# Sink attention and a feed-forward mixer on one core: zero products leave the plan and fill planned gaps of TensorE, and the whole order is searched anew

## The chip, the core and the metric

The kernel runs on one core of one Trainium2 chip. The metric is the device time of one execution in microseconds (us), as the median of several runs. Engines are called as in the profile: PE is TensorE's matmul stream and PEld its weight loads, DVE is VectorE, ACT ScalarE, POOL GpSimd, SP SyncE (here: the queue from which nearly all DMAs are issued).

## The reference

Four batches of 8 heads, 768 positions and 64 channels go through attention with 4 sink positions and a window of 128, then a low-rank mix over positions and a feed-forward layer of 512 to 2048 to 512, with a residual.

```python
scores = scale * q @ k.T                  # (4, 8, 768, 768)
keep = (pos_k < n_sink) | ((0 <= rel) & (rel < window))
a = softmax(where(keep, scores, -1e9))    # + 1e-9 under the quotient
x = (a @ v)                               # heads side by side: (4, 768, 512)
u = x + (x.T @ U @ V).T                   # U (768, 32), V (32, 768): over positions
out = u + relu(u @ w_ch1) @ w_ch2         # 512 -> 2048 -> 512
```

The weights U, V, w_ch1 and w_ch2 come as 64-bit floats and are narrowed on the chip.

## The kernel before

All of the fast path is recorded first as steps (class Plan): each step has an engine, or several that could run it, a planned duration, the tiles it reads and writes, and a priority. Tiles come from rings of buffers; the eight PSUM banks are such a ring (`self.bank`), and a step that is the first to write a bank "takes" it. `Plan.forward` then plays the steps through a list scheduler: each engine takes, at the time at which it is free, the ready step of the lowest priority number. `Plan.order` plays this some rounds, keeps the priorities of the shortest play, and applies a list of random shakes (SEEDS: a seed and a number of turns each). The steps are issued in the order of their planned starts; on the chip each engine runs its own steps in that order and waits for semaphores, so the plan fixes the order and the chip the times.

The work runs in stages on PE:

- Twelve products of a zero tile with itself (`spin`, L1643) at the start, before the branch.
- Batch 0's attention in plain 32-bit products for pairs of heads: scores (L708), softmax (L762 and L764 on DVE, L769 on ACT), transposes of the probabilities (L825), the triangular selects on POOL (L848, L851), the product with v (L732). Then the mix: transposes back to rows (L989), scaling into `wsum` (L998 on DVE), the product with U (L1000) into a bank whose copy is `t` (L521 on ACT, then the low part by the subtraction L1043 on DVE), and the product of `t` with V (L1067).
- The feed-forward layers of batches 0, 1 and 2 (L1305 to L1307 into `hh`, `hl`, then L1326), with the next batch's attention and mix woven between; batch 0's also narrows the weights, piece by piece: seven steps per piece on DVE and ACT (L115 to L123), then the halves of `w` (L521, L528). The first pieces are needed when the first feed-forward step begins.
- The last batch's feed-forward by a scheme of seven products in place of eight (L1194, L1263), and its outputs (L1282 and DMAs).

In `Fast.run`, 40 further zero products (NIDLE) are planned as ordinary steps of PE: 0.22 us each, each takes a PSUM bank of its own, priority 1e6, so that the scheduler sets one wherever PE has nothing else ready, until the 40 are used up. Each writes 128 by 128 zeros into its bank, and nothing reads them.

Of the kernel before, what the change touches and what calls it, by code (L numbers as in the profile page):

```python
# [10 lines left out]
F32 = mybir.dt.float32  # L11
# [11 lines left out]
P = 128  # L23
# [11 lines left out]
CH = 384  # L35
NCHUNK = S // CH
NBLK = CH // P
# [7 lines left out]
VC = 384  # L45
RAW = 2 * DM + 2
NSPIN = 12
NIDLE = 40
TRI = ()
ROUNDS = 10  # L50
SEEDS = ((300016, 1), (300037, 1), (300043, 1), (300076, 1), (300095, 1), (300109, 1), (300118, 1), (300125, 1), (300139, 1), (300193, 1), (300202, 1), (300209, 1), (300262, 1), (300430, 1), (300467, 1), (300473, 1), (300497, 1), (300521, 1), (300569, 1), (300586, 1), (300667, 1), (300733, 1), (300788, 1), (300838, 1), (300853, 1), (300869, 1), (300955, 1), (301207, 1), (301253, 1), (301256, 1), (301310, 1), (301379, 1), (301439, 1), (301478, 1), (301519, 1), (301685, 1), (301813, 1), (301850, 1), (301985, 1), (302191, 1), (302354, 1), (303016, 1), (303143, 1), (303320, 1), (303350, 1),)
SAME = 0.0842
PRICE = {"DVE": 3.0, "ACT": 1.5, "POOL": 1.5}
NBANK = 8
# [203 lines left out]
class Plan:  # L258
# [13 lines left out]
    def add(self, eng, dur, fn, *args, port=False, **kw):  # L272
        return self.any({eng: (dur, fn, port)}, *args, **kw)
# [102 lines left out]
    def forward(self):  # L376
        avail = dict.fromkeys(self.SYNC, 0.0)
        ready = {e: [] for e in avail}
        port = 0.0
        dma = max((-s.lat - LAND for s in self.steps if s.lat < 0.0), default=0.0)  # L380
        lanes = list(EARLY)

        def release(s):
            for e in s.ways:
                ready[e].append(s)

        def at(s, e):
            t = s.ready[e]
            if e == "SP" and s.lat >= 0.0 and len(lanes) >= NLANE:
                t = max(t, lanes[-NLANE] + 0.03)  # L390
            if s.ways[e][2]:
                t = max(t, port)
            if s.takes:
                n = len(s.takes)
                free = sorted(f[0] for f in s.takes[0].ring.free)
                return max(t, free[n - 1] if len(free) >= n else 1e12)
            return t

        def elsewhere(s, e, end):

            for x, (dur, _, _) in s.ways.items():
                if x != e:
                    t = max(avail[x], at(s, x))
                    queue = sum(o.ways[x][0] for o in ready[x]
                                if (o.prio, o.n) < (s.prio, s.n) and at(o, x) <= t and len(o.ways) == 1)
                    if t + queue + dur * PRICE[x] < end - 1e-9:
                        return True
            return False

        for s in self.steps:  # L410
            s.left, s.ready, s.heirs = len(s.deps) + len(s.after), dict.fromkeys(s.ways, 0.0), []
            for b in s.takes:
                b.ring.free = [(0.0, None, i) for i in range(b.ring.n)]
        for s in self.steps:
            if not s.left:
                release(s)
        done = 0
        while done < len(self.steps):
            turn = sorted((max(avail[e], min(at(s, e) for s in lst)), e) for e, lst in ready.items() if lst)
            turn = [x for x in turn if x[0] < 1e11] or turn  # L420
            pick = None
            for t, e in turn:
                can = sorted((s for s in ready[e] if at(s, e) <= t + 1e-9), key=lambda s: (s.prio, s.n))
# [12 lines left out]
            s.dur, s.fn, lock = s.ways[e]  # L436
            if lock:
                port = t + s.dur
            avail[e] = t + s.dur
            end = t + s.dur + s.lat  # L440
            if e == "SP" and s.lat < 0.0:
                end = -s.lat
            elif e == "SP":
                dma = max(dma, t + s.dur + BEGIN) + s.lat
                end = dma + LAND
                lanes.append(end)
            for b in s.takes:
                slot = min(b.ring.free, key=lambda f: f[0])
                b.ring.free.remove(slot)
                for x in slot[1].steps if slot[1] else ():  # L450
                    x.heirs.append(s)
                b.until, b.open, b.slot = 0.0, len(set(b.steps)), slot[2]
            for b in set(s.gives):
                b.until, b.open = max(b.until, end + 0.25), b.open - 1
                if not b.open:
                    b.ring.free.append((b.until, b, b.slot))
            for u in s.users:
                u.left -= 1
                for x in u.ways:
                    u.ready[x] = max(u.ready[x], end + self.SYNC[e][x])  # L460
                if not u.left:
                    release(u)
            for u in s.followers:
                u.left -= 1
                for x in u.ways:
                    u.ready[x] = max(u.ready[x], t)
                if not u.left:
                    release(u)
            done += 1
        self.span = max(avail.values())  # L470


def mm(n, k=1):
    return k * max(n * 1.085 + 6, 262) / 2400.0
# [18 lines left out]
class Fast:  # L493
# [197 lines left out]
    def attend_pair(self, b, pr, half, t0, qk, v, xT):  # L691
# [41 lines left out]
                        pa()[i * D:(i + 1) * D, c0 * P:(c0 + hi - lo) * P], flat()[:, at:at + D], f32(mv),  # L733
                        start=j == 0, stop=j == len(mms) - 1, skip_group_check=True)
        both = [(xT, (half, 0)), (xT, (half, 1))]
        add("PE", (0.0, 1.25, 1.50)[len(mms) - 2], run, r=ts + [t] + both, w=(pa,), prio=t0)
        self.copy(CH, lambda: xT()[:, half * CH:(half + 1) * CH], lambda: pa()[:, :CH], psum=True, r=(pa,), w=both, prio=t0)

    def scores(self, half, t0, qs, kh, kl, qbase=0, kbase=0):
# [78 lines left out]
    def transposes(self, half, t0, p, whole, own=None, late=True):  # L818
# [4 lines left out]
        def mms():  # L823
            for u in range(NBLK):
                nc.tensor.transpose(tr()[:, u * P:(u + 1) * P], p()[:, u, NS:], self.ident)  # L825
        add("PE", mm(P, NBLK), mms, r=[p] + res, w=(tr,), prio=t0)
        v3 = lambda: tr()[:, :CH].rearrange("p (u j) -> p u j", u=NBLK)
        top = lambda: res[0]()[:, :, 1, :]
        as_ = f32 if whole else lambda ap: ap
# [26 lines left out]
    def values(self, h, half, t0, t, vhl, xT):  # L856
# [4 lines left out]
        for part in range(len(t)):  # L861
            mms = []
            for kb in range(max(half * NBLK - 1, 0), (half + 1) * NBLK):
                lo = 2 * (kb - half * NBLK) + 1
                hi = min(lo + 2, 2 * NBLK)
                lo = max(lo, 0)
                mms.append((kb, lo, hi, max(kb - half * NBLK, 0)))

            def run(part=part, mms=mms):
                for i, (kb, lo, hi, c0) in enumerate(mms):  # L870
                    mv = t[part]().rearrange("p u s j -> p (u s j)")[:, lo * P:hi * P]
                    out = pa()[:, c0 * P:(c0 + hi - lo) * P]
                    st = vhl()[:, kb - kb0].rearrange("p s d -> p (s d)")
                    nc.tensor.matmul(  # L874
                        out, st, mv,
                        start=part == 0 and i == 0, stop=part == len(t) - 1 and i == len(mms) - 1,
                        skip_group_check=True)
            add("PE", (0.0, 0.275, 0.385)[len(mms) - 2], run, r=(t[part], vhl, (xT, (half, hh))), w=(pa,), prio=t0)
        dst = lambda: xT()[hh * D:(hh + 1) * D, half * CH:(half + 1) * CH]
        tb = self.tb()  # L880
        self.copy(CH, tb, lambda: pa()[D:P, :CH], psum=True, r=(pa,), w=(tb,), prio=t0)
# [61 lines left out]
    def mix_half(self, b, half, t0):  # L943
# [25 lines left out]
                pool=False, r=(tr,), w=(pst,), prio=t0)  # L969
        for pr in range(0 if native else NPAIR):  # L970
            ps = self.bank()
            add("PE", mm(CH), lambda ps=ps, pr=pr: nc.tensor.matmul(
                ps()[:, :CH], vs()[:, pr, :], pst()[:, :CH], start=True, stop=True),
                r=(vs, pst), w=(ps,), prio=t0)
            add("DVE", dve(CH), lambda ps=ps, pr=pr, sl=sl: nc.vector.tensor_tensor(
# [410 lines left out]
    def run(self):  # L1386
# [50 lines left out]
        self.bank = Ring(NBANK, lambda i: self.banks[i], free=True)  # L1437

        self.mixers()
        zero = nc.const_aps.tensor(0.0, [P, P], F32)  # L1440
        for _ in range(NIDLE):
            box = self.bank()
            self.plan.add("PE", 0.22, lambda box=box: nc.tensor.matmul(box()[:, :P], zero, zero, start=True, stop=True),  # L1443
                          w=(box,), prio=1e6)
        self.plan.lead = LEAD0
        for half in range(2):
            self.attention_halves(0, half)
# [32 lines left out]
        self.wtiles += [self.pool.tile([P, 4, DM], F32R, name=f"w{i}") for i in range(NRES + NSTREAM)]  # L1480
        for i in range(NP):
            tiles.append(self.pool.tile([P, NBLK, SW + SW], F32, name=f"p{i}"))
        with tc.manual_schedule():
            for s in order:
                s.fn()


# [246 lines left out]
```

## Time and profile before

| | |
|---|---|
| median of 3 runs | 738.07 us (737.06 to 739.82) |
| the profiled execution | 739.45 us, of which 737.7 us span from the first to the last instruction |
| PE busy | 726.3 us, 98% of the span, 4076 matmul records |
| DVE, ACT, POOL busy | 65%, 48%, 26% of the span |
| granted TensorE clock, mean | 0.996 |

The span is read in stages. A plain 32-bit matmul of the program shows as two records in the trace (a zero product too), so 40 zero products are 80 records. Successive matmuls overlap in the records, so the duration of one (399 ns for 512 columns) is longer than the distance to the next; a stretch of the timeline or of the chain of waits gives the distance.

### The profile page before, as it was taken

What the parts mean: (1) busy time and instruction counts of PE and PEld (TensorE: products, weight loads), DVE (VectorE), ACT (ScalarE), POOL (GpSimd) and SP (SyncE); (2) the same over time, 40 slices, a digit from 0 to 9 for tenths busy, and PEclk for the clock granted to TensorE, in tenths of its full rate; (3) what the DMA queues carried; (4) which work ended last, traced back from release to release, by engine and by line L of the source; (5) the groups of instructions that cost most, each with busy time, mean ns of one, the idle gap of its engine ahead of it and who ended that gap; (6) DMA issues with size and microseconds to landing.
All of it is one profiled execution on the core that took longest, in us unless ns stands there. A gap on an engine that the chain in (4) does not pass through costs nothing.

```text
span 737.7 us, 11904 instructions
## 1 busy us (share of the span) xinstructions
PE 726.3 (98%) x4076; PEld 631.4 (86%) x4076; DVE 477.5 (65%) x1343; ACT 352.9 (48%) x1026; POOL 195.3 (26%) x308
## 2 busy tenths in 40 slices
PE   9999999999999999999999999999999999999996
PEld 7678877878787999989899999999988998889895
DVE  7989788898998566578942575655679524122223
ACT  6675375675873455547641265455554222121120
POOL 4340030312431264465330045544424000000000
PEclk9999999999999999999999999999999999999999
DMA  8685767757675377554585898752368945475433
GB/s 300 229 292 203 236 241 265 251 187 265 224 264 197 110 269 255 194 187 155 196 295 176 288 323 273 268 185 80 128 204 278 316 160 200 147 290 191 171 114 119
DMA packets 45958, 160.95 MB, mean 218 GB/s; under 512 B 5056, under 2 KB 11712, under 8 KB 35648
## 3 DMA queue, kind: packets, MB, share of 16 engines
q1 hardware_dynamic: 45600, 159.71, 62.5%
q8 instruction: 34, 0.56, 0.3%
q10 hardware_dynamic: 288, 0.39, 0.2%
q14 instruction: 36, 0.29, 0.1%
HBM read 119.97 MB, written 40.11 MB: 217 GB/s over the span
## 4 chain that ended last, share of the span: by engine, by line
PE 91%; DVE 5%; DMA 2%; ACT 1%; issue 1%; DVEq 0%; ACTq 0%
PE bank L1326 25%; PE bank L1305 9%; PE bank L1306 9%; PE bank L1307 8%; PE bank L1263 8%; PE bank L1194 8%; PE bank L708 4%; PE bank L874 3%; PE bank L732 3%; PE bank L825 3%; PE bank L752 2%; PE bank L753 2%; PE bank L1443 1%; DMA w<-wd 1%; PE bank L989 1%; PE bank L1000 1%
## 5 line engine op out<-in xcount | busy, mean ns | idle before, releaser
L1326 PE MATMUL bank<-w,hh 128*128 128x512 f32 x576 | 183.5, 399 | 0.0
L1305 PE MATMUL bank<-ul,w 128*128 128x384 f32 x384 | 134.3, 350 | 0.7 <-ACT first1k L521 0.7
L1306 PE MATMUL bank<-uh,w 128*128 128x384 f32 x384 | 129.9, 338 | 0.1
L1307 PE MATMUL bank<-uh,w 128*128 128x384 f32 x384 | 129.4, 337 | 0.0
L1326 PE MATMUL bank<-w,hl 128*128 128x512 f32 x288 | 113.6, 395 | 1.0 <-DVE hl L1316 1.0
L1326 PEld LDWEIGHTS bank<-w,hh 128*128 128x128 f32 x576 | 102.9, 188 | 12.7 <-issue 1.4
L769 ACT ACTIVATE p<-p,ms 128x132 f32<-128x132 f32 x192 | 76.3, 399 | 48.9 <-DVE ms L764 48.0
L1316 DVE SCALAR_TENSOR_TENSOR hl<-bank,hh 128x384 fp32r<-128x384 f32 x96 | 53.0, 552 | 63.5 <-ACT hh L1313 63.1
L1313 ACT ACTIVATE hh<-bank 128x384 fp32r<-128x384 f32 x87 | 42.6, 489 | 80.1 <-PE bank L1307 79.3
L1305 PEld LDWEIGHTS bank<-ul,w 128*128 128x128 f32 x384 | 72.2, 188 | 9.6 <-issue 2.7
L1306 PEld LDWEIGHTS bank<-uh,w 128*128 128x128 f32 x384 | 72.3, 188 | 5.5 <-DVE w L528 0.5
L1307 PEld LDWEIGHTS bank<-uh,w 128*128 128x128 f32 x384 | 72.1, 188 | 0.0
L1326 PEld LDWEIGHTS bank<-w,hl 128*128 128x128 f32 x288 | 54.1, 188 | 14.1 <-DVE hl L1316 1.4
L764 DVE CUSTOM_DVE_ANT_0 p<-bank,mask 128x132 f32<-128x132 f32 x192 | 50.9, 289 | 13.9 <-PE bank L753 12.1
L762 DVE COPY_PREDICATED bank<-past,bank 128x128 f32<-128x128 int32 x160 | 41.9, 290 | 4.5 <-PE bank L708 3.7
L792 POOL TENSOR_TENSOR p<-p,r 128x396 f32<-128x396 f32 x16 | 14.0, 874 | 106.9 <-DVE r L780 106.8
L1263 PE MATMUL bank<-w,ul 128*128 128x512 f32 x144 | 38.5, 395 | 0.0
L769 ACT ACTIVATION_READ_ACCUMULATOR p<-p,ms 128x1 f32 x192 | 36.2, 189 | 0.0
L790 ACT ACTIVATE p<-p,r 128x132 f32<-128x132 f32 x96 | 31.4, 394 | 3.6 <-DVE r L780 3.4
L530 POOL TENSOR_TENSOR kl<-qkraw,kh 128x792 fp32r<-128x792 f32 x10 | 21.2, 2118 | 42.4 <-ACT kh L521 19.2
L848 POOL TENSOR_SCALAR_AFFINE_SELECT oph<-oph 128x256 fp32r<-128x256 f32 (+3 forms) x48 | 25.1, 523 | 24.2 <-ACT oph L521 24.1
L1263 PEld LDWEIGHTS bank<-w,ul 128*128 128x128 f32 x144 | 26.9, 188 | 5.1
(242 smaller groups left out, 1433.0 us busy)
## 6 DMA issues: line engine op xcount, KB each, us to landing
w<-wd SPq DMA_DIRECT2D x56, 1024.0 KB, 5.5
big<-in_w_dram SPq DMA_DIRECT2D x32, 512.0 KB, 4.6
wd<-w SPq DMA_DIRECT2D x16, 1024.0 KB, 4.5
big<-xd SPq DMA_DIRECT2D x33, 256.0 KB, 3.5
sd<-wsum SPq DMA_DIRECT2D x16, 512.0 KB, 7.0
w<-sd SPq DMA_DIRECT2D x8, 1024.0 KB, 5.9
qkraw<-in_kk_dram SPq DMA_DIRECT2D x16, 396.0 KB, 5.4
qkraw<-in_qq_dram SPq DMA_DIRECT2D x16, 384.0 KB, 4.4
```

Of the source, the lines that this page charges most:

```text
L762: add("DVE", dve(P), lambda: nc.vector.copy_predicated(st()[:, P + NS:UW], words(self.past), st()[:, 0:P]), w=(st,), prio=t0)
L764: add("DVE", dve(SW), lambda: nc.vector.tensor_tensor_reduce(p()[:, u, :], st()[:, wd - SW:wd], self.mask[:, min(qb, 2), :], -0.125, 3.0e3 ...
L769: add("ACT", act(SW) + 0.22, lambda: nc.scalar.activation(p()[:, u, :], p()[:, u, :], AF.Exp, bias=sm()[:, j:j + 1], scale=-1.0, accum_out ...
L790: nc.scalar.activation(p()[:, u, :], p()[:, u, :], AF.Copy, scale=r()[:, j + u:j + u + 1])
L1194: nc.tensor.matmul(out(), stat(p, dd), mv(dd), start=first and dd == 0 and k == 0, stop=dd == 1 and k == 2, skip_group_check=True)
L1263: nc.tensor.matmul(accs[k](), a()[:, sl], w()[:, m, :], start=False, stop=n == NPF - 1 and f == 1 and q == 2)
L1305: nc.tensor.matmul(ph()[:, :CH], wh, ul()[:, d, :], start=d == 0, stop=False)
L1306: nc.tensor.matmul(ph()[:, :CH], wl, uh()[:, d, :], start=False, stop=False)
L1307: nc.tensor.matmul(ph()[:, :CH], wh, uh()[:, d, :], start=False, stop=d == NC - 1)
L1313: self.plan.any({"ACT": (act(CH), lambda: nc.scalar.activation(hh(), ph()[:, :CH], AF.Relu)), "DVE": (dve(CH), lambda: nc.vector.tensor_sc ...
L1316: add("DVE", dve(CH), lambda: nc.vector.scalar_tensor_tensor(hl(), ph()[:, :CH], 0.0, f32(hh()), ALU.max, ALU.subtract), r=(ph, hh), w=(hl ...
L1326: nc.tensor.matmul(acc[k](), a()[:, sl], w()[:, m, :], start=not begin and i == 0 and j == 0, stop=i == n - 1 and j == 2)
```

## The change

The 40 planned zero products are gone from the plan. In their place the loop that issues the steps in their fixed order looks at PE's planned idle time ahead of a step: where it is 0.3 us or more (IDLE), the step takes a bank, and it starts no later than the first feed-forward step of batch 0, it issues as many zero products as go into the gap at 0.22 us each (ZERO), into the bank that the next step takes. They are no steps: the scheduler does not see them, and they hold no bank of their own.

Planned durations of five kinds of PE steps change, which moves the plan but not what a step does: the product with v of batches 0 and 1 (1.25 and 1.50 to 1.235 and 1.45 us), the transposes of the probabilities (0.327 by the formula to 0.30), the product with v of batches 2 and 3 (0.275 and 0.385 to 0.315 and 0.43), the sink product (0.176 by the formula to 0.21). The list of shakes is another one, of 133 entries where 45 stood. One loop over a set becomes a loop over the same elements in a fixed order.

```diff
-NIDLE = 40
+IDLE = 0.3
+ZERO = 0.22
-SEEDS = ((300016, 1), (300037, 1), (300043, 1), (300076, 1),
+SEEDS = ((300003, 2), (300007, 1), (300017, 1), (300027, 2),
...
-            for b in set(s.gives):
+            for b in dict.fromkeys(s.gives):
...
-        add("PE", (0.0, 1.25, 1.50)[len(mms) - 2], run, r=ts + [t] + both, w=(pa,), prio=t0)
+        add("PE", (0.0, 1.235, 1.45)[len(mms) - 2], run, r=ts + [t] + both, w=(pa,), prio=t0)
...
-        add("PE", mm(P, NBLK), mms, r=[p] + res, w=(tr,), prio=t0)
+        add("PE", 0.30, mms, r=[p] + res, w=(tr,), prio=t0)
...
-            add("PE", (0.0, 0.275, 0.385)[len(mms) - 2], run, r=(t[part], vhl, (xT, (half, hh))), w=(pa,), prio=t0)
+            add("PE", (0.0, 0.315, 0.43)[len(mms) - 2], run, r=(t[part], vhl, (xT, (half, hh))), w=(pa,), prio=t0)
...
-            add("PE", mm(CH), lambda ps=ps, pr=pr: nc.tensor.matmul(
+            add("PE", 0.21, lambda ps=ps, pr=pr: nc.tensor.matmul(
...
-        zero = nc.const_aps.tensor(0.0, [P, P], F32)
-        for _ in range(NIDLE):
-            box = self.bank()
-            self.plan.add("PE", 0.22, lambda box=box: nc.tensor.matmul(box()[:, :P], zero, zero, start=True, stop=True),
-                          w=(box,), prio=1e6)
...
+        zero = nc.const_aps.tensor(0.0, [P, P], F32)
+        until, stop = 0.0, self.marks[0][0].start
         with tc.manual_schedule():
             for s in order:
+                if s.eng == "PE":
+                    idle = s.start - until
+                    until = s.start + s.dur
+                    if s.takes and idle >= IDLE and s.start <= stop:
+                        for _ in range(int(idle / ZERO)):
+                            nc.tensor.matmul(s.takes[0]()[:, :P], zero, zero, start=True, stop=True)
                 s.fn()
```

`self.marks[0][0]` is the first feed-forward step of batch 0. PE's instructions are the same in both kernels but for the zero products: 40 before and 14 now, in three groups of 6, 3 and 5. Lines from L49 on stand one lower in the changed kernel (L825 is L826 there).

On PE, in batch 0's first attention steps, before: a product with v ends, and the zero products (`const-float32-0.0`) stand around two groups of transposes of `p`.

```order
L732 MATMUL bank_175<-opl,vhl 64x128
L1443 MATMUL bank_169<-const-float32-0.0 128x128
L1443 MATMUL bank_174<-const-float32-0.0 128x128
L1443 MATMUL bank_170<-const-float32-0.0 128x128
L1443 MATMUL bank_171<-const-float32-0.0 128x128
L1443 MATMUL bank_173<-const-float32-0.0 128x128
L825 MATMUL bank_176<-ident,p_183 128x128 x3
L1443 MATMUL bank_172<-const-float32-0.0 128x128
L1443 MATMUL bank_169<-const-float32-0.0 128x128
L825 MATMUL bank_174<-ident,p_183 128x128 x3
L1443 MATMUL bank_170<-const-float32-0.0 128x128
L1443 MATMUL bank_175<-const-float32-0.0 128x128
```

The same place in the changed kernel, from the product with v to the spreading of V (L586).

```order
L733 MATMUL bank_173<-opl,vhl 64x128
L826 MATMUL bank_171<-ident,p_185 128x128 x3
L826 MATMUL bank_175<-ident,p_183 128x128 x3
L826 MATMUL bank_172<-ident,p_183 128x128 x3
L1488 MATMUL bank_176<-const-float32-0.0 128x128 x5
L586 MATMUL bank_176<-big_112,pick 128x192 x2
L960 MATMUL bank_169<-ident,first0q 128x128 x3
L586 MATMUL bank_174<-big_112,pick 128x192 x2
```

Where 17 zero products stood between this product with v and the first L585, 5 stand now, all ahead of the step that needs the narrowed U and V, and into that step's bank.

On DVE, the steps just ahead of the subtraction that ends `t` of batch 0 (L1043 before); `bank<-big` and `bank<-nr` rows are pieces of the weights' narrowing, one `big` buffer each.

```order
L123 TENSOR_TENSOR bank_169<-nr,bank_169 128x512
L120 SCALAR_TENSOR_TENSOR nr<-big_114,nr 128x512
L998 TENSOR_TENSOR wsum<-bank_170,rs 128x512
L998 TENSOR_TENSOR wsum<-bank_173,rs 128x512
L121 TENSOR_SCALAR nr<-nr 128x512
L998 TENSOR_TENSOR wsum<-bank_171,rs 128x512
L122 SCALAR_TENSOR_TENSOR bank_174<-big_114,nr 128x512
L528 TENSOR_TENSOR w_179<-bank_169,w_179 128x512
L123 TENSOR_TENSOR bank_174<-nr,bank_174 128x512
L117 TENSOR_SCALAR nr<-nr 128x512
L118 TENSOR_SCALAR nr<-nr 128x512
L1043 TENSOR_TENSOR t<-bank_172,t 32x512
```

And in the changed kernel (L1044).

```order
L999 TENSOR_TENSOR wsum<-bank_169,rs 128x512
L999 TENSOR_TENSOR wsum<-bank_172,rs 128x512
L118 TENSOR_SCALAR nr<-nr 128x512
L999 TENSOR_TENSOR wsum<-bank_174,rs 128x512
L529 TENSOR_TENSOR w_179<-bank_171,w_179 128x512
L121 SCALAR_TENSOR_TENSOR nr<-big_114,nr 128x512
L123 SCALAR_TENSOR_TENSOR bank_173<-big_112,nr 128x512
L122 TENSOR_SCALAR nr<-nr 128x512
L124 TENSOR_TENSOR bank_173<-nr,bank_173 128x512
L1044 TENSOR_TENSOR t<-bank_170,t 32x512
```

The weight piece in `big_114` had its two long steps (L122, L123) ahead of `t` before, and has them behind it now; over the whole list nine DVE steps fall away ahead of `t`, and four short ones come in.

On PE, where batch 1's mix ends and `t` times V (L1067) is added to it, before.

```order
L1067 MATMUL bank_173<-vst,t 128x384
L1067 MATMUL bank_170<-vst,t 128x384
L1067 MATMUL bank_172<-vst,t 128x384
L1326 MATMUL bank_174<-w_181,hh 128x512 x2
L1326 MATMUL bank_174<-w_181,hl 128x512
L1067 MATMUL bank_170<-vst,t 128x384
L1067 MATMUL bank_172<-vst,t 128x384
L1067 MATMUL bank_173<-vst,t 128x384
L1067 MATMUL bank_170<-vst,t 128x384
L1067 MATMUL bank_172<-vst,t 128x384
L1326 MATMUL bank_176<-w_180,hh 128x512 x2
```

And in the changed kernel (L1068), from the fourth of the eight products on.

```order
L1068 MATMUL bank_169<-vst,t 128x384
L1068 MATMUL bank_171<-vst,t 128x384
L1327 MATMUL bank_176<-w_179,hh 128x512 x2
L1327 MATMUL bank_176<-w_179,hl 128x512
L1068 MATMUL bank_175<-vst,t 128x384
L1068 MATMUL bank_172<-vst,t 128x384
L1306 MATMUL bank_170<-ul,w_179 128x384
L1307 MATMUL bank_170<-uh,w_179 128x384
L1308 MATMUL bank_170<-uh,w_179 128x384
L1068 MATMUL bank_171<-vst,t 128x384
```

Five of the eight stood in one run; now no more than three stand together, with feed-forward products between.

## Rows read from the trace of the kernel before

**Rows 1.** Page, parts 1 and 2: engines, and slices of the span.

```profile
PE 726.3 (98%) x4076; PEld 631.4 (86%) x4076; DVE 477.5 (65%) x1343; ACT 352.9 (48%) x1026; POOL 195.3 (26%) x308
PE   9999999999999999999999999999999999999996
PEclk9999999999999999999999999999999999999999
```

**Rows 2.** Page, part 4: shares of the chain that ended last.

```profile
PE 91%; DVE 5%; DMA 2%; ACT 1%; issue 1%; DVEq 0%; ACTq 0%
```

**Rows 3.** Waits of PE, whole span: who was waited for, total, times, longest.

```profile
PE bank L1326 <- DVE hl L1316: 1.0, 1, 1.0
PE bank L708 <- DVE ms L764: 0.9, 1, 0.9
PE spin L1643 <- PEq L1716: 0.8, 1, 0.8
PE bank L1067 <- DVE t L1043: 0.8, 1, 0.8
PE bank L1305 <- ACT first1k L521: 0.7, 1, 0.7
PE bank L989 <- DVE w L528: 0.5, 1, 0.5
PE bank L825 <- ACT p L790: 0.3, 1, 0.3
```

**Rows 4.** Busy time by stretch: PE, PEld, DVE, ACT, POOL, granted clock, DMA.

```profile
0.00:66.40 66.40, 64.55 (x465) 49.20 (x466) 58.11 (x224) 45.89 (x157) 21.93 (x59) 0.97 0.79 275
29.00:32.40 3.40, 3.40 (x18) 1.92 (x14) 2.70 (x18) 3.05 (x12) 0.00 (x0) 0.50 0.29 83
66.40:200.00 133.60, 133.60 (x748) 107.91 (x747) 115.03 (x329) 83.67 (x241) 28.21 (x48) 1.00 0.67 227
731.90:737.70 5.80, 0.00 (x1) 0.00 (x0) 0.74 (x2) 0.00 (x0) 0.00 (x0) 0.82 0.41 146
```

**Rows 5.** Chain of waits, 0 to 70 us, in order of time: start, length, what.

```profile
17.50 1.31 PE bank L1443 x10
...
19.91 2.01 PE bank L1443 x18
```

**Rows 6.** PE's timeline: start, length, instruction, idle time before it.

```profile
27.92 0.70 PE L708 MATMUL bank<-kh,qs 64*128 64x260 f32 x2 [0.89 <-DVE ms L764]
...
30.47 2.09 PE L708 MATMUL bank<-kh,qs 64*128 64x260 f32 x8
...
224.40 2.30 PE L1067 MATMUL bank<-vst,t 128*128 128x384 f32 x5
226.54 0.63 PE L1326 MATMUL bank<-w,hh 128*128 128x512 f32 x2
228.12 0.50 PE L1326 MATMUL bank<-w,hl 128*128 128x512 f32 x1 [0.95 <-DVE hl L1316]
```

**Rows 7.** DVE's groups, 0 to 66.4 us: count, busy us, mean ns, idle before.

```profile
L122 DVE SCALAR_TENSOR_TENSOR bank<-big,nr 128x512 f32<-128x512 uint32 x5 | 4.0, 798 | 0.2
L123 DVE TENSOR_TENSOR bank<-nr,bank 128x512 f32<-128x512 bf16 x5 | 3.4, 688 | 0.0
L528 DVE TENSOR_TENSOR w<-bank,w 128x512 fp32r<-128x512 f32 x5 | 3.4, 687 | 0.7 <-ACT w L521 0.7
L117 DVE TENSOR_SCALAR nr<-nr 128x512 bf16<-128x512 bf16 (+1 forms) x7 | 2.5, 356 | 0.0
L118 DVE TENSOR_SCALAR nr<-nr 128x512 uint16<-128x512 uint16 (+1 forms) x4 | 1.4, 361 | 0.1
L528 DVE TENSOR_TENSOR vsh<-xhl,vsh 32x512 fp32r<-32x512 f32 x2 | 1.4, 686 | 0.1
L123 DVE TENSOR_TENSOR big<-nr,big 128x384 f32<-128x384 bf16 x1 | 0.8, 754 | 0.0
L522 DVE COPY xT<-big 128x192 f32<-128x192 f32 x1 | 0.7, 660 | 0.0
L522 DVE CAST ust<-big 128x192 fp32r<-128x192 f32 x1 | 0.6, 569 | 0.0
```

More of the change, by code (lines that the diff above doesn't have):

```diff
@@ L47 @@
 NSPIN = 12
-NIDLE = 40
+IDLE = 0.3
+ZERO = 0.22
 TRI = ()
 ROUNDS = 10
-SEEDS = ((300016, 1), (300037, 1), (300043, 1), (300076, 1), (300095, 1), (300109, 1), (300118, 1), (300125, 1), (300139, 1), (300193, 1), (300202, 1), (300209, 1), (300262, 1), (300430, 1), (300467, 1), (300473, 1), (300497, 1), (300521, 1), (300569, 1), (300586, 1), (300667, 1), (300733, 1), (300788, 1), (300838, 1), (300853, 1), (300869, 1), (300955, 1), (301207, 1), (301253, 1), (301256, 1), (301310, 1), (301379, 1), (301439, 1), (301478, 1), (301519, 1), (301685, 1), (301813, 1), (301850, 1), (301985, 1), (302191, 1), (302354, 1), (303016, 1), (303143, 1), (303320, 1), (303350, 1),)
+SEEDS = ((300003, 2), (300007, 1), (300017, 1), (300027, 2), (300028, 1), (300095, 1), (300099, 2), (300169, 1), (300127, 1), (300229, 1), (300140, 1), (300166, 1), (300182, 1), (300353, 1), (300200, 1), (300445, 1), (300343, 1), (300461, 1), (300427, 1), (300529, 1), (300422, 1), (300587, 1), (300685, 1), (300851, 1), (300955, 1), (300826, 1), (300884, 1), (300916, 1), (301180, 1), (301499, 1), (301261, 1), (301238, 1), (301246, 1), (301667, 1), (301414, 1), (301481, 1), (301685, 1), (302419, 1), (301834, 1), (302164, 1), (302582, 1), (302932, 1), (303683, 1), (302782, 1), (303767, 1), (303256, 1), (303170, 1), (303392, 1), (303461, 1), (303641, 1), (304471, 1), (303910, 1), (304381, 1), (304852, 1), (305512, 1), (306041, 1), (306221, 1), (305746, 1), (306511, 1), (306689, 1), (307249, 1), (307669, 1), (306958, 1), (307282, 1), (307490, 1), (308516, 1), (309389, 1), (310051, 1), (309656, 1), (309554, 1), (310799, 1), (311431, 1), (311197, 1), (310808, 1), (310714, 1), (310894, 1), (311396, 1), (312161, 1), (311434, 1), (312112, 1), (312661, 1), (313171, 1), (312929, 1), (314291, 1), (313880, 1), (315007, 1), (313486, 1), (314824, 1), (315535, 1), (316373, 1), (315010, 1), (318371, 1), (319493, 1), (321761, 1), (323149, 1), (323816, 1), (331118, 1), (332959, 1), (334003, 1), (338548, 1), (340469, 1), (340555, 1), (341147, 1), (342566, 1), (344965, 1), (344464, 1), (347642, 1), (362093, 1), (359687, 1), (391331, 1), (401470, 1), (421820, 1), (436081, 1), (434359, 1), (449086, 1), (458353, 1), (449503, 1), (477169, 1), (479365, 1), (514921, 1), (515137, 1), (497614, 1), (504859, 1), (510979, 1), (521800, 1), (526561, 1), (539101, 1), (541085, 1), (548660, 1), (561265, 1), (581803, 1), (588457, 1), (581762, 1),)
```

## The prediction, on record before the changed kernel ran

> **What bounds the kernel now.** I read the engines' shares and the slices first: PE is busy 98% of the span, in every slice but the last, and its clock is granted in full nearly throughout [rows 1]. The chain that ended last is PE's to 91% [rows 2]. So a change counts if it takes work off PE, takes a wait of PE away, or brings one. Next I read PE's own waits: over the whole span they are 5.0 us, in seven places [rows 3]. Then the stretches. From 66.4 us, where the first feed-forward step begins, to 200 us PE is busy 133.60 of 133.60 us [rows 4]: nothing is to be won there, since the change leaves PE's products the same but for the zero products. What is left is (a) the first 66.4 us, where PE's busy time holds zero products and DVE is busy 58.11 us, 88% [rows 4]; (b) the ends of batches 0 and 2, where PE waits for DVE; (c) the last 5.8 us, outputs after the last matmul [rows 4].
>
> **Zero products.** Two groups of the chain have 10 and 18 records, so 5 and 9 products, in 1.31 and 2.01 us [rows 5]: 3.32 us for 14, 0.237 us each. There are 26 fewer: 6.2 us of PE's time go. They stood where PE had nothing else, so what is late next is what PE would have waited for: DVE's softmax and copies, and ACT and POOL behind them. From below the gain is nothing (each product becomes a wait of its length), from above 6.2 us.
>
> **The wait at 27.0 us and what follows it.** PE waits 0.89 us for DVE, to 27.92 us [rows 6], and from 29.0 to 32.4 us the granted clock is 0.50, the 1.2 GHz level [rows 4]; the 3.4 us there hold what 1.7 us at 2.4 GHz hold, so it costs 1.7 us of PE. Together 2.6 us that a new order may avoid, or repeat. [...]
>
> **DVE ahead of `t`.** Batch 0's feed-forward can't begin before DVE's subtraction into `t`. In the new order nine DVE steps stand behind it, or on ACT or POOL: one each of the narrowing's L122 (4.0 / 5 = 0.80 us), L123 (3.4 / 5 = 0.68) and 384-column L123 (0.8), of L117 (2.5 / 7 = 0.36) and L118 (1.4 / 4 = 0.35), of the halves of `w` (0.68) and `vsh` (0.70), the cast to `ust` (0.6) and the copy to `xT` (0.7): 5.7 us [rows 7]. Four short ones come in; no row here shows them all, I estimate them at L117's 0.36, 1.4 us. So DVE's work ahead of `t` falls by about 4.2 us. If DVE idles as long as before (66.4 - 58.11 = 8.3 us [rows 4]), `t` and the feed-forward come 4.2 us earlier, and PE, 8.8 us ahead by the two items above (6.2 + 2.6), waits for it. If DVE idles less, the gain grows, at the most to those 8.8 us; if PE's waits simply take the products' place, it shrinks to nothing. I take 4.2, since DVE at 88% is the row that lies nearest. What went behind `t` has cover: between 66.4 and 200 us DVE is busy 115.03 of 133.60 us, so 18.6 us are free [rows 4]; were the first weights late, PE would stand for the length of their last steps, up to L122 and L123 and both halves, 0.80 + 0.68 + 2 x 0.68 = 2.8 us.
>
> **The ends of batches.** At the end of batch 0 five products `t` times V stand in a run: from 224.40 to 226.54 us, 2.14 us [rows 6]. Each frees its bank by an addition on DVE, and PE goes at DVE's pace; a free product of 384 columns is about 0.18 us, from the feed-forward's 133.60 us for 748 records of 384 and 512 columns and others [rows 4], so 1.2 us are lost. Then L1326 waits 0.95 us for DVE, which still had the additions ahead of `hl` [rows 6]. In the new order there is no such run: the eight stand in groups of 3, 2, 2 and 1 with feed-forward products between. From above: these 2.2 us and the other waits behind 66.4 us (0.8 + 0.7 + 0.5 + 0.3 [rows 3]) all go, 4.5 us. From below: they go and others like them come in an order that was never run, and 2.3 us more than before, the price of the 0.8, 0.7, 0.5 and 0.3 doubled. I take 1.8 us: the run and half of the 0.95 behind it, the rest as before.
>
> **Nothing elsewhere.** The corrected durations and the fixed loop order change no instruction; they act through the order alone, which I have counted. In the tail, the last DVE addition (0.74 us busy after 731.9 [rows 4]) and an output DMA follow the last matmul, in both orders; there I cost nothing, since the last two banks end further apart than before and no more work follows.
>
> **Sum.** 4.2 + 1.8 = 6.0 us. The profiled execution takes 739.45 us (span 737.7, 1.7 around it): 733.4 by its measure. It lies 1.4 us above the median of the three runs, 738.07, so in medians 732.1 us.
>
> **The rivals.**
> 1. *More than this.* DVE idles little in the shorter start, PE keeps the whole 8.8 us, and the ends of batches lose their 2.2 to 4.5 us: 11.0 to 13.3 us, 724.8 to 727.1 us. For it: PE has no other work that could be in the way. Against it: DVE would have to be busy 58.11 - 4.2 = 53.9 of 57.6 us, 94%, where it has 88% now and waits for PE and ACT in between.
> 2. *The waits take the products' place.* The zero products only covered waits for the chain PE, DVE, ACT, POOL, PE of a pair of heads; this chain is as long as before, whatever stands in the gaps. Then the start gives 0 to 2 us and the ends of batches 0 to 1.8: 734.3 to 738.1 us, I set 736.5. For it: 40 products fitted in because PE had nothing to do. Against it: DVE's work ahead of `t` does fall. That the change doesn't do what it says comes out here too: the new products are written to the bank of the next step; had that step waited for the bank itself, they would start only when it is free and stand ahead of the step, at most 14 x 0.237 = 3.3 us late: 735.4 us.
> 3. *Slower, by the clock.* PE's gaps in the first 60 us are no longer filled where the chip's waits differ from the plan's, and after them the clock falls as it did at 29.0 us. The waits give the 6.2 us back, and each stretch like that one costs 1.7 us. One is in the time already; with three or more in its place it is 3.4 us and more slower: 741.5 us for three, 743.2 for four. It decides from the third stretch on, in the first 60 us. For it: the wait at 27.92 us is unfilled and was followed by such a stretch. Against it: the gaps that the plan knows of are still filled, and the wait of 0.95 us later cost no clock.
>
> **How the numbers follow.** Forecast 0.48, with a range of its own from 729 to 735; rival 1 0.13; rival 2 0.28; rival 3 0.11. A difference under 0.5% (3.7 us; the three runs lie 2.8 us apart) can't be told from no change. Faster by more, under 734.4 us: nine tenths of the forecast, all of rival 1 and a tenth of rival 2, 0.59. Within: the rest of the two and a fifth of rival 3, 0.32. Slower, over 741.8 us: 0.09. For 8 in 10, I leave out the better half of rival 1 and the longer part of rival 3: 727 to 740 us.
>
> **What would show it.** Right: 28 records of zero products; the first feed-forward product near 62 us in place of 66.4; DVE busy about 54 us until then, 87%; no run of five `t` times V at DVE's pace near 215 us; 66 to 200 us as solid as before. PE's waits in the first 60 us should be 2 to 5 us in all, most of them for DVE or for POOL's selects. Rival 1 shows the first feed-forward product before 59 us, rival 2 at 64 us or later with as much idle time on PE as products went. Rival 3 shows a granted clock of 0.5 in three or more stretches ahead of 60 us. I am wrong in the step on DVE if DVE's idle time in the start grows by as much as its work fell, and in the step on the ends if the waits behind 200 us add up to more than the 3.3 us of before.

## The result, and the profile after

The changed kernel takes 727.02 us (median of 4 runs, 726.99 to 727.45), the kernel before 738.71 beside it (737.06 to 739.82): a ratio of 0.9845, with a 95% interval of 0.9824 to 0.9866, so 11.7 us less. The prediction said 732.1 and 727 to 740: the direction is right, and the size is that of the lower edge: the measured gain is nearly twice the forecast of 6.0 us. The time is rival 1's, "more than this".

I read the page of the changed kernel first, its parts 1 and 2 (engines, then PE and its granted clock in 40 slices), to be held against [rows 1]:

```profile
PE 716.0 (99%) x4024; PEld 625.4 (86%) x4024; DVE 474.8 (65%) x1341; ACT 350.3 (48%) x1016; POOL 205.6 (28%) x314
PE   8999999999999999999999999999999999999996
PEclk9999999999999999999999999999999999999998
```

There are 52 matmul records fewer (26 products), and PE's busy time is 10.3 us less. The profiled execution took 727.0 us, with a span of 725.3. PE's waits over the whole span (who was waited for, total, times, longest) come next:

```profile
PE spin L1647 <- PEq L1720: 0.8, 1, 0.8
PE bank L709 <- DMA kh<-in_k_dram: 0.7, 1, 0.7
PE bank L709 <- PE spin L1647: 0.5, 1, 0.5
PE bank L1327 <- ACT hh L1314: 0.4, 1, 0.4
PE bank L1327 <- DVE hl L1317: 0.2, 1, 0.2
PE bank L1327 <- DVE ms L765: 0.2, 1, 0.2
```

They are 2.8 us where [rows 3] add up to 5.0, and the ones behind the start are three short ones, 0.8 us, for 3.3. Then busy time by stretch (PE, PEld, DVE, ACT, POOL, granted clock, DMA), in the stretches of [rows 4], the start cut at the changed kernel's own first feed-forward product, which stands at 58.23 us (66.47 before):

```profile
0.00:54.78 54.78, 52.78 (x384) 38.41 (x385) 49.17 (x210) 40.97 (x149) 24.67 (x58) 1.00 0.85 290
0.00:58.20 58.20, 56.20 (x407) 41.70 (x408) 52.53 (x216) 43.93 (x156) 24.67 (x58) 1.00 0.86 295
29.00:32.40 3.40, 3.40 (x31) 2.35 (x25) 3.40 (x22) 3.40 (x15) 1.27 (x4) 1.00 0.66 212
58.20:200.00 141.80, 141.22 (x792) 113.15 (x791) 124.11 (x351) 86.84 (x246) 31.45 (x51) 1.00 0.68 234
```

The stretch from 29.0 to 32.4 us has the clock at 1.00 (0.50 before). The first row ends where the subtraction into `t` begins, at 54.78 us. Before, it began at 61.77 us, and the same row of that kernel reads:

```profile
0.00:61.77 61.77, 59.92 (x434) 44.72 (x435) 53.55 (x215) 42.76 (x150) 21.93 (x59) 0.97 0.79 276
```

DVE's work ahead of `t` fell from 53.55 to 49.17 us, by 4.4, and its idle time from 8.2 to 5.6, by 2.6. What it no longer waits for is seen in DVE's waits of that stretch; first those of before (0 to 66.4 us), then those of the changed kernel (0 to 58.2 us):

```profile
DVE bank L762 <- PE bank L708: 1.6, 3, 0.7
DVE rs L811 <- ACT rs L808: 1.0, 1, 1.0
DVE w L528 <- ACT w L521: 0.7, 1, 0.7
DVE p L764 <- PE bank L708: 0.7, 1, 0.7
DVE wsum L998 <- PE bank L989: 0.3, 1, 0.3
```

```profile
DVE p L765 <- PE bank L709: 0.8, 2, 0.7
DVE bank L763 <- PE bank L709: 0.4, 2, 0.2
DVE p L765 <- POOL oph L852: 0.4, 1, 0.4
```

2.6 us of waits for PE became 1.2, and 1.7 us of waits for ACT none; one for POOL, 0.4 us, came in. (Two waits at the very start, for a DMA and for POOL, stand in both kernels.)

The first feed-forward product stands at 58.23 us, but it isn't the same point of the work as at 66.47 us before. PE's timeline of the changed kernel, first around its first zero products, then behind that product:

```profile
8.64 1.60 PE L1488 MATMUL bank<-const-float32-0.0 128*128 128x128 f32 x12
10.93 0.93 PE L709 MATMUL bank<-kh,qs 64*128 64x132 f32 x8 [0.68 <-DMA kh<-in_k_dram]
...
58.23 0.38 PE L1306 MATMUL bank<-ul,w 128*128 128x384 f32 x1
...
58.80 0.49 PE L1060 MATMUL bank<-ident,wsum 128*128 128x128 f32 x3
59.05 0.42 PE L1066 MATMUL bank<-xhl,vsh 128*128 128x384 f32 x1
59.31 0.34 PE L1068 MATMUL bank<-vst,t 128*128 128x384 f32 x1
...
60.01 0.40 PE L1341 MATMUL bank<-vsh,xhl 128*128 128x512 f32 x1
```

The last four rows, six records, stood ahead of the first feed-forward product before, and stand behind it now; all other records but the zero products are the same. They take 0.9 us from one start to the next. So of the 8.2 us by which that product comes earlier, 7.3 are won at equal work, and 0.9 is work put behind it.

The whole account on PE: the last matmul ends at 719.10 us where it ended at 731.90, 12.8 us earlier. By the distances from one start to the next, the zero products are 6.0 us of this (80 records in 9.5 us before, 28 in 3.5 after, without the 0.68 us of waiting for the DMA above, which is in the list of waits), PE's listed waits 2.2 (5.0 less 2.8) and the stretch at half clock 1.7. The run of five products of [rows 6] went, some 1.2 us. About 1.7 us are left, in short distances and in no listed wait, that I can't assign. At equal work 7.3 of the 12.8 us are there at the first feed-forward product: 6.0 and 1.7, less 0.2 us by which the waits grew there, give them within 0.2. The other 5.5 come behind it, and what I can't assign is there. The tail after the last matmul grew by 0.35 us, to 6.2.

### The profile page after: what moved, and what is told of

It is laid out like the page before. It is cut to its first block, busy times and chain, and to the rows that moved or that the text cites. A ratio compares the mean times of both kernels' runs of the same rounds, so it can differ in the third digit from the quotient of the medians.

```text
span 725.3 us, 11806 instructions
## 1 busy us (share of the span) xinstructions
PE 716.0 (99%) x4024; PEld 625.4 (86%) x4024; DVE 474.8 (65%) x1341; ACT 350.3 (48%) x1016; POOL 205.6 (28%) x314
## 4 chain that ended last, share of the span: by engine, by line
PE 91%; DVE 4%; DMA 2%; ACT 1%; issue 1%; SPq 0%; POOL 0%; DVEq 0%; ACTq 0%; POOLq 0%
PE bank L1327 26%; PE bank L1264 9%; PE bank L1306 9%; PE bank L1307 9%; PE bank L1308 9%; PE bank L1195 8%; PE bank L709 3%; PE bank L875 3%; PE bank L826 3%; PE bank L733 3%; PE bank L753 2%; PE bank L754 1%; PE bank L990 1%; DMA big<-in_w_dram 1%; PE bank L1001 1%; DMA xd<-big 1%
## 5 line engine op out<-in xcount | busy, mean ns | idle before, releaser
L793 POOL TENSOR_TENSOR p<-p,r 128x396 f32<-128x396 f32 x17 | 16.8, 987 | 79.2 <-DVE r L781 79.2
L522 ACT COPY tb<-bank 64x384 f32<-64x384 f32 x32 | 15.0, 475 | 34.9 <-PE bank L875 34.7
L791 ACT ACTIVATE p<-p,r 128x132 f32<-128x132 f32 x87 | 28.5, 394 | 5.8 <-DVE r L781 5.6
```

What stands on the lines that cost most here:

```text
L791: nc.scalar.activation(p()[:, u, :], p()[:, u, :], AF.Copy, scale=r()[:, j + u:j + u + 1])
```

## The experiments

Every run was timed beside runs of the kernel before on the same chip; ratios are to these, with 95% intervals.

**1. Products out, order kept.** Theory A: the products are work that is paid for. Theory B: they cover waits, and the order has to change. The kernel before, its 40 planned steps kept in the plan but issuing nothing:

```diff
-self.plan.add("PE", 0.22, lambda box=box: nc.tensor.matmul(box()[:, :P], zero, zero, start=True, stop=True),
+self.plan.add("PE", 0.22, lambda: None,
```

> The kernel before in its own order, with the 40 zero products left out of the instructions (their output is never read, so the result is unchanged). Theory A (each product took PE time that the path had to pay): 40 x 0.237 = 9.5 us less PE work, so 729 to 732 us against 738.7. Theory B (the products only covered waits; the gain of the change is its new order): waits of the same length take their place, 736.5 to 739 us. Theory C (they keep the clock up): waits unfilled and two or more further stretches of granted clock 0.5 before 60 us, at 1.7 us each: 741 us or more.

Measured: 737.66 us (10 runs, 735.32 to 739.95), ratio 0.9976 (0.9964 to 0.9989). So 9.5 us of products are worth 1.2 us by the medians, 0.8 to 2.7 by the interval. PE's waits show where they went, the first four of the list, and then two stretches with the granted clock of each behind POOL's busy time:

```profile
PE bank L959 <- ACT first0q L521: 1.9, 1, 1.9
PE bank L1000 <- DVE wsum L998: 1.2, 1, 1.2
PE bank L1326 <- DVE hl L1316: 1.0, 1, 1.0
PE bank L825 <- ACT p L769: 0.9, 2, 0.4
```

```profile
20.80:27.60 6.80, 6.15 (x21) 4.20 (x23) 6.58 (x15) 3.50 (x9) 3.01 (x5) 0.50 0.34 112
225.60:232.40 6.80, 6.18 (x17) 5.51 (x18) 4.96 (x10) 1.78 (x3) 0.00 (x0) 0.50 0.18 58
```

The waits ahead of the first feed-forward product are 6.6 us (1.7 before), and it begins only 1.1 us earlier, at 65.42. (This profiled execution took 739.95 us, the longest of the ten, with a mean clock of 0.988, where the other nine have 0.994 to 0.997.) Theory A falls: in the old order rival 2, "the waits take the products' place", is what happens, with some of rival 3's clock.

**2. The changed kernel without its 14 products**, and **3. with 40**, in the same three gaps:

```diff
-for _ in range(int(idle / ZERO)):
+for _ in range(0):
```

```diff
-for _ in range(int(idle / ZERO)):
+for _ in range({6: 17, 3: 9, 5: 14}[int(idle / ZERO)]):
```

> The changed kernel in its own order without its 14 zero products (result unchanged). A: 14 x 0.24 = 3.3 us less, 723.7 us against 727.0. B: waits in their place, 726.5 to 727.5. C: at least one stretch of clock 0.5 before the feed-forward, 728.5 us or more.

> The changed kernel in its own order, its three groups of 6, 3 and 5 zero products lengthened to 17, 9 and 14 (40, as many as before; result unchanged). A: 26 x 0.237 = 6.2 us more, 733.2 us. B as I hold it (the order has little room left): most of it is paid too, 4 to 6 us, 731 to 733; B with much room: under 2 us, 727 to 729. So it tells how much wait the new order still hides, not A from B.

Measured: 727.68 us (4 runs, 725.55 to 729.18), ratio 0.9834 (0.9809 to 0.986), without products; 729.93 (729.10 to 731.34), ratio 0.9881 (0.9859 to 0.9902), with 40. PE's longest wait without products, and the stretch behind it:

```profile
PE bank L709 <- DVE ms L765: 2.7, 1, 2.7
```

```profile
10.90:17.70 6.80, 6.50 (x29) 4.40 (x31) 3.08 (x23) 4.39 (x19) 2.87 (x9) 0.50 1.01 381
```

The 2.7 us stand where the changed kernel has six products and a wait of 0.7. The 6.8 us behind them are at the lower level: the 33 records from 11.20 us on take 7.1 us to the start of the next, and the same 33 in the changed kernel, from 10.93 us on, 4.1. In this execution (729.18 us, mean clock 0.993) the first feed-forward product came 3.2 us later than in the changed kernel; the execution with a mean clock of 1.000 took 725.55 us, less than any of the changed kernel's. The median lies between theory B and theory C, and theory A falls: the 14 products gain nothing that the medians can tell. The execution with the lowest mean clock is the longest of the four, that with the highest the shortest; with the products the four runs lie within 0.5 us of each other. With 40, the products take 5.7 us more (9.2 where the 14 take 3.5); the first feed-forward product comes 3.7 us later and the median is 2.9 us longer: about half of what is added is paid, which lies between the two expectations. With experiment 1 this tells what the number of products is worth in one and the same order: 1.2 us for 40 taken out of the old order, 2.9 for 26 put into the new one, where the whole change gains 11.7.

**4. The new way with the old durations and the old 45 shakes.** Three of its edits (the transposes' and the sink product's durations go back likewise):

```diff
-SEEDS = ((300003, 2), (300007, 1), (300017, 1), (300027, 2),
+SEEDS = ((300016, 1), (300037, 1), (300043, 1), (300076, 1),
...
-        add("PE", (0.0, 1.235, 1.45)[len(mms) - 2], run, r=ts + [t] + both, w=(pa,), prio=t0)
+        add("PE", (0.0, 1.25, 1.50)[len(mms) - 2], run, r=ts + [t] + both, w=(pa,), prio=t0)
...
-            add("PE", (0.0, 0.315, 0.43)[len(mms) - 2], run, r=(t[part], vhl, (xT, (half, hh))), w=(pa,), prio=t0)
+            add("PE", (0.0, 0.275, 0.385)[len(mms) - 2], run, r=(t[part], vhl, (xT, (half, hh))), w=(pa,), prio=t0)
```

> The changed kernel's way of filling gaps, but with the planned durations and the 45 shakes of the kernel before: no zero products in the plan, 23 of them in gaps of the fixed order (result unchanged). A: the gain is there without the new search, 727 to 731 us. B: it isn't, 733 to 739 us, since the shakes were found for another plan.

Measured: 748.58 us (747.75 to 753.32), ratio 1.0148 (1.0111 to 1.0185). It is slower than before, which neither theory had. Behind the first feed-forward product PE waits 8.2 us; the first four of the list:

```profile
PE bank L1327 <- DVE hl L1317: 1.8, 2, 1.6
PE bank L973 <- ACT first1k L522: 1.2, 1, 1.2
PE bank L1001 <- DVE wsum L999: 1.2, 1, 1.2
PE spin L1647 <- PEq L1720: 0.8, 1, 0.8
```

This list of shakes fits its own plan only: by the planner's own measure these 45 take this plan from 710.4 to 727.2 us, where they took the old one from 712.6 to 711.5. The list can't be undone by itself, so experiments 8 to 10 compare whole searches.

**5. and 6. What sets the changed kernel's start.** Theory D: DVE's queue. Theory P: PE's. Either got needless work ahead of the first feed-forward product, spread evenly: ten additions on DVE (`junk` from a constant tile; 0.38 us each on average in the trace, where 0.21 was expected), or nine more zero products on PE.

```diff
+                if s.eng == "DVE" and s.start <= stop:
+                    nd += 1
+                    if nd % 11 == 0 and nd <= 110:
+                        nc.vector.tensor_tensor(junk, self.past, self.past, ALU.add)
```

```diff
+                if s.eng == "PE" and s.start <= stop and s.takes:
+                    np_ += 1
+                    if np_ % 7 == 0:
+                        nc.tensor.matmul(s.takes[0]()[:, :P], zero, zero, start=True, stop=True)
```

> The changed kernel with 10 needless DVE additions of 128 columns (0.21 us each, 2.1 us in all) spread over the DVE steps ahead of the first feed-forward step; result unchanged. Theory D (in the changed order DVE's queue sets the start: 52.6 of 58.2 us busy): the first feed-forward product comes 1.6 to 2.1 us later and the time is 728.6 to 729.2 us against 727.0. Theory P (PE's queue sets it): under 0.7 us. Theory X (they bind in turns): 0.8 to 1.5 us.

> The changed kernel with 9 further zero products on PE (0.237 us each, 2.1 us in all), one ahead of every seventh step that takes a bank before the first feed-forward step, outside the planned gaps; result unchanged. D: they are hidden, under 0.7 us, 727.0 to 727.7. P: 1.6 to 2.1 us, 728.6 to 729.2. X: 0.8 to 1.5 us in both this run and the one with DVE's load. Run e3's 26 products (6.2 us) moved the first feed-forward product by 3.65 us.

Measured: DVE load 728.89 us (728.61 to 729.17), ratio 0.9865 (0.9848 to 0.9881), 1.9 us more than the changed kernel; PE load 727.57 (727.02 to 728.76), ratio 0.9853 (0.9837 to 0.987), 0.5 more. The times speak for D. The traces are less plain. The stretch up to the first feed-forward product, first of the DVE load and then of the PE load:

```profile
0.00:59.80 59.80, 57.47 (x408) 42.26 (x408) 54.79 (x227) 44.24 (x157) 24.93 (x58) 1.00 0.83 288
```

```profile
0.00:60.15 60.15, 58.72 (x425) 43.89 (x426) 52.75 (x217) 44.38 (x157) 24.34 (x58) 1.00 0.84 289
```

Both loads move that product, by 1.6 and by 1.9 us from 58.23. DVE's busy time up to it rose by 2.3 us with the first load, and by 0.2 with the second. DVE's idle time went the other way: 5.7 us in the changed kernel, 5.0 with the DVE load, 7.4 with the PE load. So needless work on PE makes DVE wait. But the delay from the PE load is given back: at 142 us, where the changed kernel waits 0.4 us for ACT and this run doesn't, 1.3 us are left of it, at the last matmul 0.7. That from the DVE load grows to 2.4, and 0.7 of this comes between 500 and 600 us, far behind the additions. So in the new order PE and DVE are both near the limit in the start, and the first feed-forward product by itself isn't the time: what DVE loses lasts here, what PE loses is partly won back. Theory D fits the times, not that product; with one trace of each, that DVE alone sets the start isn't shown.

**7. The additions behind the run of five.** The kernel before, with batch 1's eight additions that free the banks of `t` times V cut from 384 to 32 columns. It leaves out the rest of that sum, so its output isn't the reference's.

```diff
+                sh = slice(sl.start, sl.start + 32) if b == 1 else sl
...
-                    x()[:, sl], x()[:, sl], pu()[:, :CH], ALU.add), r=(pu,), w=parts, prio=t0)
+                    x()[:, sh], x()[:, sh], pu()[:, :sh.stop - sh.start], ALU.add), r=(pu,), w=parts, prio=t0)
```

> The kernel before in its own order, with batch 1's eight DVE additions behind t times V cut from 384 to 32 columns (the rest of the sum is left out). My step on the ends of batches: the run of five products takes about 0.9 us in place of 2.14 and the wait of 0.95 us for hl behind it is gone or under 0.4: 1.5 to 2.2 us less in the trace at 224 to 229 us, 736.5 to 737.5 us. Rival (the wait hangs on the weights' narrowing in DVE's queue, not on the additions): the run shortens, the wait stays or grows, and the feed-forward behind waits as long: within 0.6 us of the kernel before.

Measured: 737.45 us (10 runs, 735.37 to 738.59), ratio 0.998 (0.9971 to 0.999): 1.5 us less, 0.7 to 2.1 by the interval. PE's timeline there, to be held against the last three of [rows 6]:

```profile
222.66 1.30 PE L1067 MATMUL bank<-vst,t 128*128 128x384 f32 x5
223.80 0.63 PE L1327 MATMUL bank<-w,hh 128*128 128x512 f32 x2
224.71 0.50 PE L1327 MATMUL bank<-w,hl 128*128 128x512 f32 x1 [0.28 <-DVE hl L1317]
```

The five go through in 1.14 us (2.14 before), and the wait behind them is 0.28 us (0.95): 1.7 us at this place. The prediction's working for this run, 1.2 and half of 0.95, was right in sum.

**8. to 10. Three ways, one search.** Theory S: what makes the gain is the search, not the way of filling (O) or the corrected durations (U). Each kernel got its own search of 4000 shakes, and a shake was kept if it shortened the planner's own length. Apart from what is named, only the list differs; the line of experiment 10 stands for all three:

- 8 (s1): the kernel before, with its products as steps (and the loop of fixed order); 14 shakes kept, planned length 709.3 us.
- 9 (s2): the changed kernel with the old durations, as in experiment 4; 13 kept, 708.1 us.
- 10 (s3): the changed kernel; 29 kept, 706.8 us.

```diff
-SEEDS = ((300003, 2), (300007, 1), (300017, 1), (300027, 2),
+SEEDS = ((900003, 1), (900018, 1), (900024, 1), (900047, 1),
```

> The plan of the kernel before (40 zero products as steps, old durations), with a search of its own: 4000 random shakes, each kept if the planned span fell. Same effort for the next two runs. Theory O (the products out of the plan make the gain): this one is 4 us or more slower than both others. Theory S (what counts is how long one searches, and the 133 kept shakes against 45 are the gain): the three lie within 3 us of each other, all between 730 and 742 us. Theory U (the corrected durations make the gain, as the plan then matches the chip): this and the second alike, the third 4 us or more faster. One search each, so 2 us of luck between them mean nothing.

> The changed kernel's way (products in the gaps of the fixed order, none in the plan), with the old durations, and 4000 shakes of its own. O: 4 us or more under the first, like the third. S: within 3 us of both. U: like the first, 4 us or more over the third.

> The changed kernel in all but its shakes: 4000 shakes of the same search. O: like the second. S: within 3 us of both, and 3 to 8 us over the changed kernel with its 133. U: 4 us or more under both others, near the changed kernel (727 to 730).

Measured: 734.87 us (733.49 to 735.66), ratio 0.9953 (0.9937 to 0.997); 736.58 (733.16 to 738.80), ratio 0.996 (0.9944 to 0.9975); 736.24 (733.26 to 741.0), ratio 0.9978 (0.9953 to 1.0002). The three lie within 3 us of each other, as theory S has it, and the third is 9.2 us above the changed kernel, where 3 to 8 were expected. Neither the way of filling nor the durations give the gain by themselves. PE's waits in 8, and the first three in 10:

```profile
PE spin L1643 <- PEq L1716: 0.8, 1, 0.8
PE bank L989 <- ACT xT L521: 0.4, 2, 0.3
PE bank L1015 <- ACT first1k L521: 0.4, 1, 0.4
PE bank L708 <- DVE ms L764: 0.3, 1, 0.3
PE bank L959 <- ACT first0q L521: 0.2, 1, 0.2
```

```profile
PE bank L1016 <- ACT xhl L522: 2.9, 2, 1.7
PE spin L1647 <- PEq L1720: 0.8, 1, 0.8
PE bank L1017 <- DVE xhl L529: 0.5, 2, 0.3
```

8 hardly waits any more, no longer than the changed kernel, and its last matmul ends 7.4 us later, with the 40 products in its way (10.0 us, 6.5 more than the 14). 10 has only the 14 and waits again, twice for ACT at the ends of batches, and after the second time the clock falls for 3.4 us; its last matmul ends 9.1 us later, of which waits are 3.1 and the clock 1.7, and 3.9 stand in short distances that I can't assign (traces of the changed order, experiments 2, 3, 5 and 6, differ in such a rest by as much). By these traces, one search each, the gain needs both: products out of the path, and an order in which little waits in their place.

**11. and 12. How much of the list.** The planned length is 711.5 us for the kernel before and 704.6 for the changed one, but of the 133 shakes 74 leave it as it was and 21 lengthen it. Theories: L, the planned length decides; M, the list was kept for more than that, each entry gave a little; N, few shakes do with the new way. The changed kernel with the first 45 entries (planned 709.0 us), and with the first 90 (705.8 us):

> The changed kernel with the first 45 of its 133 shakes, as many as the kernel before has. 16 zero products in groups of 6, 6, 3 and 1. The planner's own length of the whole is 708.97 us here, 704.60 with all 133, 711.50 in the kernel before, and 706.75 in s3, which took 736.2 us. Theory L, the planned length decides, and each kernel's shakes are only a way to it: h45 lies with s2 (planned 708.1, 736.6 us measured) and s3, at 735 to 738 us. Theory M, the 133 were kept for more than the planned length (two in three of them leave it as it was or lengthen it), and each gave a little on the chip: h45 has some third to two thirds of the gain of 11.7 us, 731 to 735 us. Theory N, the way of filling and the corrected durations give the gain with few shakes, and the rest of the list gives little: 727 to 730 us.

> The changed kernel with the first 90 of its 133 shakes; 14 zero products in groups of 6, 3 and 5 as with all of them. Planned length 705.84 us, 1.25 us over that of all 133 and 0.9 us under that of s3 (736.2 us measured). Theory L, the planned length decides: just under s3, 734 to 736 us. Theory M, every shake gave a little on the chip: 728 to 730 us. Theory N: 727 to 728 us.

Measured: 730.23 us (729.63 to 730.7), ratio 0.9886 (0.9869 to 0.9902), and 729.44 (728.28 to 729.92), ratio 0.9876 (0.9859 to 0.9892). Theory L falls: experiment 10 is planned 2.2 us shorter than the first of these, and takes 6.0 us longer on the chip. 8.3 us of the gain are there with 45 entries, as many as the kernel before has; the other 88 bring 3.2. The first lies between M and N, the second is as M has it, and theory S falls in part: the length of the search isn't what counts. What the entries were chosen by, the kernel doesn't show; that stays open. None of these kernels beats the changed one.

## Why the prediction was right, and where it was too small

**The range, by luck.** It ends at 727, and 727.02 was measured; the forecast's own range, 729 to 735, was missed. What follows tells where the other 5.7 us of the 11.7 came from.

**The products, right in both bounds.** The sum's ends were 0 and 6.2 us. In the old order 40 of them give 1.2 us (experiment 1), in the new one the 26 are 6.0 us of PE's account, and the waits of the start grew by only 0.2. That "what is late next is what PE would have waited for" decides it is what experiments 1 and 8 show from two sides.

**The wait at 27.0 us and the half clock: right.** Both are gone. The half clock's 1.7 us are as priced: the 16 records from 29.04 to 32.49 us before take 3.45 us, and records of the same kinds at the full clock 1.8. Of the 0.89 us of waiting nothing is left in the sum, since 1.1 us of other waits came in the start, for `spin` and the DMA. Which wait is followed by a fall of the clock, the runs leave open. With waits of 1.9, 1.0 and 2.7 us in experiments 1 and 2 came 6.8 us at the 1.2 GHz level. After waits of 0.7 and 0.4 us in the changed kernel and the 0.95 us of [rows 6] came none, nor after one of 2.7 us in experiment 9, behind which the granted clock is 1.00:

```profile
377.71 0.50 PE L1016 MATMUL bank<-xhl,ust 128*128 128x512 f32 x1 [2.74 <-ACT xhl L522]
```

The Trainium skill ("TensorE: Matmul & The Clock Gate", section on HAM oscillation) tells of a kernel whose waits for DMAs are each long enough for PE to be throttled, so that every next burst starts cold. No trace here shows such a series.

**The step that failed: "If DVE idles as long as before".** The step on DVE ahead of `t` was right in its work, 4.2 us predicted and 4.4 measured, and wrong in the sentence behind it. DVE's idle time fell by 2.6 us, since 1.4 us of its waits for PE and 1.7 for ACT went, and 0.4 for POOL came. I had counted PE's shorter start only as something that waits for DVE, but DVE had waited for PE as well, 2.6 us in the list of before above; rival 1 names such waits, the sum left them out. Experiment 6 shows the same from the other side: with work added on PE, DVE's idle time grows by 1.7 us. From `t` to the first feed-forward product another 1.3 us went (4.7 to 3.45 us), but 0.9 of it is the work that now stands behind that product, so 0.3 are won. 4.4 + 2.6 + 0.3 make the 7.3 us at equal work, toward the upper end of 8.8, where 4.2 stood in the sum. DVE at 88% was no floor: it is at 90% now (52.53 of 58.20 us).

**The ends of batches: mis-sized.** Taken 1.8 us, measured 5.5 at equal work behind the first feed-forward product, above the upper end (4.5). The run of five was sized right (experiment 7). "The rest as before" was wrong: all the waits there went from 3.3 us to 0.8, and 1.8 us are in small distances whose cause stays open. In the changed kernel the eight products stand in groups with others between:

```profile
222.30 0.68 PE L1068 MATMUL bank<-vst,t 128*128 128x384 f32 x3
...
223.34 0.51 PE L1068 MATMUL bank<-vst,t 128*128 128x384 f32 x2
...
224.38 0.50 PE L1068 MATMUL bank<-vst,t 128*128 128x384 f32 x2
...
225.25 0.34 PE L1068 MATMUL bank<-vst,t 128*128 128x384 f32 x1
```

**The tail, right in kind:** nothing gained, 0.35 us lost in this execution. With the same order it is 5.5 to 6.0 us in experiments 2, 3, 5 and 6, so the 0.35 may be chance.

**What would show it.** 28 records: yes. 66 to 200 us solid: nearly, 141.22 of 141.80 us. First feed-forward near 62: no, 58.2, which was rival 1's sign (before 59), though at equal work it is 59.1. DVE near 54 us: 52.5. Waits of 2 to 5 us in the start: 2.0, most of them not for DVE or POOL but at the very start and for a DMA. Rival 2 is what the old order does without its products.

## What to carry to other kernels

What filler work on the bounding engine costs depends on the order around it: taken out of an order made with it, it turned into waits and a lower clock (1.2 of 9.5 us were won), and added to one made without it, about half of it was paid. When two engines wait for each other in a stretch, price its shortening by both engines' waits: idle time of the one that looks like the bound shrank here together with the other's work. Before a product's start time is read as a gain, count whether the same work stands ahead of it in both orders. A plan's own length didn't rank these orders on the chip; a few of them have to be run.

## What the runs showed of the hardware

- While work ran, the stretches at half clock were 3.4 us long in two profiles (before at 29.0 us, experiment 10 at 551.4) and 6.8 us in the three of experiments 1 and 2. Waits of about the same length, 0.95 us before and 0.96 in experiment 1, at the same place in the program, were followed by none and by one of 6.8 us; so were waits of 2.7 us, in experiments 9 and 2.
- The kernel before differs from execution to execution with its clock: nine with a mean granted clock of 0.999 took 738.0 us on average, thirteen with 0.996 took 739.5.
- Orders differ in how far their runs spread, by more than their planned lengths do: the changed kernel's four lie within 0.5 us, the ten of experiment 10 within 7.7 us (its longest had a mean clock of 0.992, its shortest 0.999).
